# FFN rows turned by small DMAs in place of matmuls, down weights in four loads each, and an earlier row choice

## The chip, the cores and the metric

The kernel runs on one core of one Trainium2 chip. The metric is the device time of one execution in microseconds (us). Of the kernel before, three executions gave 251.94, 251.48 and 251.61 us, so the median is 251.61.

## The reference

One layer takes x (2048 tokens, 1024 features) and mixes two branches per token. Cut to what matters:

```python
g = sigmoid((x * gate_w).sum(-1, keepdims=True))       # one gate per token
q, k, v = split(x @ wqkv)                              # 32 heads of 32
pq, pk = phi(q), phi(k)                                # phi(t) = (t + 1 if t > 0 else exp(t)) + 1e-6
kv, z = sum_s(pk * v), sum_s(pk)
a = (pq @ kv) / (pq @ z + 1e-6) @ wo                   # linear attention
r = x @ w_r                                            # router
i = argmax(r)                                          # one row of 2048 is chosen
y = (silu(x[i] @ w_gate) * (x[i] @ w_up)) @ w_down     # FFN of this one row, 3584 wide
b = x;  b[i] += y * sigmoid(r[i])
out = g * a + (1 - g) * b
```

The FFN has three weight matrices of 7.3 MB each in bf16 and one row to multiply, so it is a matter of loading weights beside the attention's matmuls.

## The kernel before, in words

**Units.** The tokens are cut into 16 tiles of 128 (t = 0 to 15). A unit is eight matmuls of 128x512 into one PSUM buffer. `unit_KV(t, nb)` makes a quarter of k and v of tile t (nb 0 and 1: k, 2 and 3: v). `unit_Q(g, j)` makes a piece of q. k and q units are drained by two ScalarE activations (`u`, then `e`) and one VectorE step that writes `pk` or `pq_all`; v units by one ScalarE copy. Four PSUM buffers (`ps_work`) rotate among the units, so TensorE can start a unit once the unit some four places earlier is drained. `unit_KVACC(t)` adds pk and v of a tile into two accumulators; it runs for four tiles at a time, after the second unit of t = 8 and 12 and after the last tile. The tiles `pk` and `vt` have five buffers; GpSimd presets a column of each `vt` (a memset), and waits for that until `unit_KVACC` has freed the buffer.

**The order.** A loop over t from 4 to 15 emits four KV units and then a number of Q units per tile (`Q_PER_T`). Between the units it emits the FFN's work by tables: `GU_AFTER`, `GATE_STEPS`, `DOWN_STEPS`, `FLUSH_AFTER`. A place (t, i) is after KV unit i for i of 0 to 3, after Q unit i - 4 for i from 4 on, and "end" is the end of the tile. The helper `in_order` pins instructions to program order only while `strict[0]` is true. It is set false before the router, and from there on a scheduler chooses the place of most instructions in each engine's list by its own estimate of when inputs are ready; once built, each list runs as it stands.

**Row choice.** `router_part1` finds the best row on VectorE (`rmax`, `idx_i`), and GpSimd fetches that row (`xsel_row`, `xsel4`). `router_part2` turns it into columns on TensorE (`xs_ps`), copied to `xs_f` and `xs_pad`. The first weight load waits for the row fetch.

**FFN pieces.** All FFN weights come as pieces through one pool `ffw` of nine buffers, loaded on SP's queue in the order of `ffn_pieces`; a piece is loaded when the piece nine places earlier has been used.
- The first 2048 gate columns (half 0; four groups of 512) are multiplied on VectorE in 16 steps of 128x1024 (`gate_rows`, summed in `gacc`) and reduced over the partitions by TensorE (`gate_reduce`, `gps`).
- The up columns of half 0, and gate and up of half 1 (1536 columns) go over TensorE (`gate_up`): four matmuls side by side in 32 columns each, result on partitions 0, 32, 64 and 96 of one bank of `ps_ffn`. This pool has one buffer.
- `finish_gate` takes silu over a whole 128x512 tile (Exp on ScalarE, add, reciprocal and product on VectorE), though only four of its rows count. `finish_up` makes `h_bf`, and `h_transpose` brings h to 128 partitions with four or three matmuls against `sel4` into `hps`, copied to `hcol`.
- The 3584 rows of w_down are 28 slices of 128 rows, two per piece (`down_rows`); each slice is one VectorE step of 128x1024 into `yacc`, which is the first half of `gacc`. A piece is one load of 512 KB, in rows of 2 KB.
- `down_finish` sums `yacc` over the partitions on TensorE (`yps`), forms the row `brow` on VectorE and writes it into `xp`, a copy of x in DRAM made on SP's queue behind the down loads.

**After the FFN.** `zcol`, `kvbd` and `zc` are taken from the accumulators. `den_group` computes the denominators (`dps` on TensorE, `dn` on ScalarE, `rd` on VectorE); `unit_kvT` transposes kv (`pt`), `unit_M` multiplies with wo (`pm`), 15 more Q units run between, and the last loop makes the output tiles (`ot`). The tiles of this stage take over SBUF space of the earlier one: `dn` and `rd` may be written only when the transfer out of `brow` has landed. The third `pt` matmul needs a PSUM bank after `dn` has read it.

Of the kernel before, what the change touches and what calls it, by code (L numbers as in the profile page):

```python
# [13 lines left out]
BF = mybir.dt.bfloat16  # L14
F32 = mybir.dt.float32
I32 = mybir.dt.int32
U32 = mybir.dt.uint32
ALU = mybir.AluOpType
ACTF = mybir.ActivationFunctionType
# [3 lines left out]
P = 128  # L23
# [7 lines left out]
LN1EPS = math.log1p(EPS)  # L31
N_WARM = 6
Q_PER_T = {4: 2, 5: 1, 6: 1, 7: 2, 8: 1, 9: 1, 10: 2, 11: 1, 12: 1, 13: 1, 14: 1, 15: 0}
GU_AFTER = {(7, "end"): 4, (9, 1): 4, (10, 3): 8, (12, 1): 8}
FLUSH_AFTER = {(9, 3), (13, 0)}
GATE_STEPS = {6: 5, 7: 6, 8: 5}
M_AFTER = {3: (0, 0), 6: (0, 1), 9: (1, 0), 12: (1, 1)}
DOWN_STEPS = {10: (1, 1, 1, 1, 1, 1), 11: (1, 1, 1, 1, 1), 12: (1, 0, 1, 1, 1), 13: (1, 1, 1, 1, 1), 14: (1, 1, 1, 1, 1), 15: (1, 1, 1)}
FFN_DEPTH = 9
NORM_PER_T = [3, 2, 0, 2, 2, 2, 2, 2, 2, 2, 2, 0, 0, 0, 0, 0]  # L40

# [2 lines left out]
def kernel(  # L44
# [13 lines left out]
    nc = tc.nc  # L58
# [5 lines left out]
    const = ctx.enter_context(tc.tile_pool(name="const", bufs=1))  # L64
# [8 lines left out]
    strict = [True]  # L73
# [81 lines left out]
    nc.gpsimd.memset(one_bf[:], 1.0)  # L155
    ones_row = const.tile([1, P], BF)
    nc.gpsimd.memset(ones_row[:], 1.0)
    sel4 = const.tile([P, 4], BF)
    nc.gpsimd.memset(sel4[:], 0.0)
    for j in range(4):  # L160
        nc.gpsimd.memset(sel4[32 * j : 32 * j + 1, j : j + 1], 1.0)
    off16_i = const.tile([P, 1], I32)
    nc.gpsimd.iota(off16_i[:], pattern=[[0, 1]], base=0, channel_multiplier=16)
    wrg_pad = const.tile([P, KC, 32], BF)
# [3 lines left out]
    hcol = rt.tile([P, 28], F32)  # L168
# [193 lines left out]
    def router_part2():  # L362
        xs_ps = ps_ffn.tile([P, KC + 1], F32, tag="f")
        for c in range(KC):
            pe.matmul(xs_ps[:, c : c + 1], lhsT=xsel_row[0:1, c * P : (c + 1) * P], rhs=one_bf[0:1, 0:1],
                             start=True, stop=True)
        pe.matmul(xs_ps[:, KC : KC + 1], lhsT=ones_row[0:1, :], rhs=rmax_bf[0:1, 0:1], start=True, stop=True)
        dve.tensor_copy(xs_f[:], xs_ps[:, 0:KC])
        dve.tensor_copy(xs_pad[:, :, 0], xs_ps[:, 0:KC])
        act.activation(sig[:], xs_ps[:, KC : KC + 1], ACTF.Exp, scale=-1.0)  # L370
        dve.tensor_scalar_add(sig[:], sig[:], 1.0)
        dve.reciprocal(sig[:], sig[:])
    ffw = phq.enter_context(tc.tile_pool(name="ffw", bufs=FFN_DEPTH, side="right"))
    h_bf = [rt.tile([P, 512], BF, name=f"h_bf{i}") for i in range(2)]
    sg_t = [rt.tile([P, 512], F32, name=f"sg{i}") for i in range(2)]
    ffn_state = {}

    def gate_up_load(half, wmat, c):
# [8 lines left out]
        ffn_state["last_ld"] = ld  # L387
        return wt

    def finish_gate(half, ps, w):  # L390
        eg = tmp.tile([P, 512], F32, tag="ffn_e", bufs=1)
        act.activation(eg[:, 0:w], ps[:, 0:w], ACTF.Exp, scale=-1.0)
        dve.tensor_scalar_add(eg[:, 0:w], eg[:, 0:w], 1.0)
        dve.reciprocal(eg[:, 0:w], eg[:, 0:w])
        dve.tensor_tensor(sg_t[half][:, 0:w], ps[:, 0:w], eg[:, 0:w], op=ALU.mult)

    def finish_up(half, ps, w):
        dve.tensor_tensor(h_bf[half][:, 0:w], ps[:, 0:w], sg_t[half][:, 0:w], op=ALU.mult)

        def h_transpose():  # L400
            hps = ps_ffn.tile([P, 16], F32, tag="f")
            nb = w // P
            for b in range(nb):
                pe.matmul(hps[:, 4 * b : 4 * b + 4], lhsT=h_bf[half][:, b * P : (b + 1) * P], rhs=sel4[:], start=True, stop=True)
            dst = hcol[:].rearrange("p (j b) -> p j b", b=7)[:, :, 4 * half : 4 * half + nb]
            src = hps[:, 0 : 4 * nb].rearrange("p (b j) -> p j b", j=4)
            dve.tensor_copy(dst, src)

        ffn_state["pending"] = h_transpose

    def gate_up(half, which):
        w = 512 if half == 0 else 384
        for wi in which:
            wmat = (B_w_gate, B_w_up)[wi]
            for c in range(KC):
                def load(wmat=wmat, c=c):
                    return gate_up_load(half, wmat, c)

                def compute(wt, wi=wi, c=c):
                    if c == 0:  # L420
                        ps = ps_ffn.tile([P, 512], F32, tag="f")
                        ffn_state["ps"] = ps
                    ps = ffn_state["ps"]
                    for j in range(4):
                        pe.matmul(ps[32 * j : 32 * j + 32, 0:w], lhsT=xs_pad[:, c, :], rhs=wt[:, w * j : w * j + w],
                                  start=(c == 0), stop=(c == KC - 1), tile_position=(0, 32 * j))
                    if c == KC - 1:
                        (finish_gate, finish_up)[wi](half, ps, w)

                yield load, compute  # L430

# [14 lines left out]
    def gate_reduce():  # L446
        ps = ps_red.tile([P, 512], F32, name="gps")
        for j in range(4):
            pe.matmul(ps[32 * j : 32 * j + 32, :], lhsT=ones_f[:], rhs=gacc[:, 512 * j : 512 * j + 512],
                      start=True, stop=True, tile_position=(0, 32 * j))  # L450
        finish_gate(0, ps, 512)

    def down_rows():
        wdv = B_w_down.rearrange("(k p) n -> p k n", p=P)
        pairs = [(7 * j + b, 1) for b in (0, 2) for j in range(4)]
        pairs += [(7 * j + 4, 1) for j in range(4)] + [(6, 7), (20, 7)]
        for i2, (k0, dk) in enumerate(pairs):
            def load(k0=k0, dk=dk):
                wt = ffw.tile([P, 2048], BF, tag="ffw")
                ld = nc.sync.dma_start(out=wt[:].rearrange("p (k n) -> p k n", k=2), in_=wdv[:, k0 : k0 + dk + 1 : dk, :])  # L460
                tc.add_manual_dep(ld.ins, ffn_state["last_ld"].ins.name, NOSYNC, reason="queue order")
                ffn_state["last_ld"] = ld
                return wt

            def compute(wt, kk, i2=i2, k0=k0, dk=dk):
                w, h1 = wt[:, 1024 * kk : 1024 * kk + 1024], hcol[:, k0 + dk * kk : k0 + dk * kk + 1]
                if i2 == 0 and kk == 0:
                    dve.tensor_scalar(yacc, w, h1, None, op0=ALU.mult)
                else:
                    dve.scalar_tensor_tensor(yacc, w, h1, yacc, op0=ALU.mult, op1=ALU.add)  # L470

            yield load, compute
# [21 lines left out]
    def ffn_pieces():  # L494
        g0, u0, gu, dn = gate_rows(), gate_up(0, (1,)), gate_up(1, (0, 1)), down_rows()
        yield from islice(g0, 6)
        yield from islice(u0, 4)
        yield from g0
        yield from u0
        for n in (2, 4):  # L500
            yield from islice(dn, n)
            yield from islice(gu, 8)
        yield from dn
        yield from wo_pieces()

    pieces = ffn_pieces()
    inflight = deque()

    def ffn_prefetch():
        while len(inflight) < FFN_DEPTH:  # L510
            nxt = next(pieces, None)
            if nxt is None:
                return
            inflight.append((nxt[0](), nxt[1]))

    def ffn_flush():
        pend = ffn_state.pop("pending", None)
        if pend is not None:
            pend()

    def ffn_step(n):
        for _ in range(n):
            wt, comp = inflight.popleft()
            comp(wt)
            ffn_prefetch()
# [18 lines left out]
    def down_finish():  # L544
        ps = ps_ffn.tile([P, 256], F32, tag="f", name="yps")
        for j in range(4):
# [4 lines left out]
        nc.gpsimd.dma_start(out=xp[bass.ds(nonlocal_idx[0], 1), :].rearrange("o (j n) -> (o j) n", j=4),  # L551
                            in_=brow[0:128:32, :])

    q_units = deque((g, j) for j in range(4) for g in range(NG))
    for t in range(4):
        unit_KVACC(t)
    for t in range(4, NT):
        for nb in range(4):
            unit_KV(t, nb)
            if nb == 1 and t > 4 and t % 4 == 0:  # L560
                for t0 in range(t - 4, t):
                    unit_KVACC(t0)
            ffn_step(GU_AFTER.get((t, nb), 0))
            if (t, nb) in FLUSH_AFTER:
                ffn_flush()
            gate_step(int(nb < GATE_STEPS.get(t, 0)))
            steps = DOWN_STEPS.get(t, ())
            if nb < len(steps):
                down_step(steps[nb])
        for i in range(Q_PER_T[t]):  # L570
            unit_Q(*q_units.popleft())
            gate_step(int(4 + i < GATE_STEPS.get(t, 0)))
            if 4 + i < len(steps):
                down_step(steps[4 + i])
            if t == 4 and i == 0:
                router_part1()
                ffn_prefetch()
        if t == 5:
            router_part2()
        ffn_step(GU_AFTER.get((t, "end"), 0))  # L580
        if t == 8:
            gate_reduce()
    unit_Q(*q_units.popleft())
# [164 lines left out]
```

## Time and profile before

| what | value |
|---|---|
| median of three executions | 251.61 us |
| profiled execution, its own time | 251.87 us |
| span of its profile, first to last instruction | 250.1 us |
| TensorE busy | 244.7 us, 1602 matmuls |
| VectorE, ScalarE, GpSimd busy | 163.1, 125.8, 51.9 us |
| DMA: moved, mean rate | 47.73 MB, 191 GB/s |
| down loads: 14 of 512 KB, issue to landing (median) | 5.8 us |
| `wo` loads on SP: 8 of 128 KB, issue to landing (median) | 2.8 us |
| matmuls into `hps`, chain of waits | 0.08 us (four) and 0.05 us (three) |
| reciprocals of `finish_gate` on VectorE | 3.35 and 2.55 us |

The profile is of one execution and lies 0.26 us above the median. Its time is the span and 1.8 us around it. A group line names the engine, the operation, out<-in by the program's names, the shape and the count, then busy time and the mean of one in ns. In the timeline, a line has the start in us, the length, engine, operation, and in brackets the idle time of the engine before it and what ended that. The view of waits has: who waited <- for whom: us in total, times, longest. The chain in order of time has: start, length, what. L80 is the helper that records the order, so instructions are told apart by their tiles.

### The profile page before, as it was taken

The page shows a single profiled execution, that of the slowest core. Times are in us where ns is not written, and L with a number is a line of the kernel's source. Part 1 is how long each engine was busy: PE and PEld are TensorE (multiplying, and loading weights), DVE is VectorE, ACT ScalarE, POOL GpSimd, SP SyncE. Part 2 cuts the span into 40 slices and gives each one's busy share as a digit, 9 for nine tenths or more (in the row PEclk, how much of TensorE's full clock was granted, in tenths as well). Part 3 has the DMA queues.
Part 4 walks back from the last instruction along what each step waited for, and adds up shares of the span by engine and source line. Part 5 has one row for each costly group of instructions (what it writes and reads, how often), then busy time and mean ns, then how long its engine had stood idle before and what let it go on. Part 6 is the DMA issues. An engine that isn't in the chain of part 4 may idle for free.

```text
span 250.1 us, 4197 instructions
## 1 busy us (share of the span) xinstructions
PE 244.7 (98%) x1602; PEld 111.1 (44%) x1602; DVE 163.1 (65%) x257; ACT 125.8 (50%) x200; POOL 51.9 (21%) x102
## 2 busy tenths in 40 slices
PE   7999999999999999999999999999999999999994
PEld 3444454444444434444544444444444444444442
DVE  0045015326999288699689993585878999953442
ACT  2096235556545364564535554568887633333210
POOL 5000001010000100000132000210666689950000
PEclk9999999999999999999999999999999999999999
DMA  6999990019999928499699996230000564454122
GB/s 199 303 340 225 258 334 26 0 27 320 350 348 272 340 58 250 146 338 327 194 292 300 457 349 134 70 132 1 3 0 5 171 210 144 161 175 144 66 84 84
DMA packets 47242, 47.73 MB, mean 191 GB/s; under 512 B 18732, under 2 KB 35380, under 8 KB 47160
## 3 DMA queue, kind: packets, MB, share of 16 engines
q1 hardware_dynamic: 46552, 46.29, 60.7%
q0 software_dynamic: 640, 1.19, 1.8%
q8 instruction: 12, 0.20, 0.3%
q14 instruction: 6, 0.05, 0.1%
q10 hardware_dynamic: 32, 0.00, 0.0%
HBM read 39.34 MB, written 8.40 MB: 191 GB/s over the span
## 4 chain that ended last, share of the span: by engine, by line
PE 95%; DMA 2%; SPq 1%; DVE 0%; issue 0%; DVEq 0%
PE ps L80 88%; PE first L80 2%; DMA wkv<-in_A_wqkv_dram 2%; PE kvacc L80 2%; PE dps L80 1%; PE rps L80 1%; SPq L80 1%; PE pm L80 1%; PE gps L80 0%; DVE ot L80 0%; PE yps L80 0%; PE xs_ps L80 0%; DVEq L743 0%; PE pt L80 0%; PE hps L80 0%
## 5 line engine op out<-in xcount | busy, mean ns | idle before, releaser
L80 PE MATMUL ps<-wkv,xT 128*128 128x512 bf16 x480 | 106.5, 379 | 0.0
L80 PEld LDWEIGHTS <-xT 128*128 128x128 bf16 x512 | 49.3, 98 | 60.5 <-issue 2.6
L80 PE MATMUL ps<-xT,wq 128*128 128x512 bf16 x256 | 58.4, 379 | 0.0
L80 PE MATMUL ps<-m_sb,pq_all 128*128 128x512 bf16 (+2 forms) x264 | 55.6, 373 | 0.0
L80 ACT ACTIVATE u<-ps 128x512 f32<-128x512 f32 x60 | 35.9, 599 | 36.5 <-PE ps L80 35.8
L80 ACT ACTIVATE e<-u 128x512 f32<-128x512 f32 x64 | 40.4, 632 | 2.0
L646 POOL TENSOR_TENSOR pq_all<-pq_all,rb 128x512 bf16<-128x512 bf16 x32 | 36.6, 1163 | 14.4 <-DVE rb L80 13.9
L80 PEld LDWEIGHTS <-pq_all 128*128 128x128 bf16 x264 | 25.5, 98 | 30.2 <-issue 0.4
L80 PEld LDWEIGHTS <-wq 128*128 128x128 bf16 x256 | 24.3, 98 | 30.2 <-issue 2.1
L80 DVE SCALAR_TENSOR_TENSOR pq_all<-ps,e 128x512 bf16<-128x512 f32 x32 | 22.0, 686 | 23.6 <-ACT e L80 23.5
L80 DVE SCALAR_TENSOR_TENSOR gacc<-wt,hcol,gacc 128x1024 f32<-128x1024 bf16 x27 | 34.6, 1281 | 4.1 <-DMA wt<-in_B_w_down_dram 3.7
L80 ACT CAST vt<-ps 128x512 bf16<-128x512 f32 x32 | 18.9, 589 | 32.8 <-PE ps L80 32.8
L80 DVE SCALAR_TENSOR_TENSOR ot<-ps,gate,xg 128x512 bf16<-128x512 f32 (+2 forms) x33 | 23.6, 724 | 15.1 <-PE ps L80 14.2
L80 ACT ACTIVATE xg<-xt,omg 128x1024 f32<-128x1024 bf16 x16 | 18.2, 1148 | 25.8 <-DVE ot L80 25.8
L80 DVE SCALAR_TENSOR_TENSOR pk<-ps,e 128x512 bf16<-128x512 f32 x28 | 19.1, 686 | 7.5 <-ACT e L80 7.5
L209 POOL MEMSET vt<- 128x16 bf16 x16 | 2.4, 200 | 101.8 <-PE kvacc L80 101.3
L80 DVE STREAM_SHUFFLE rb<-rdp 128x512 f32<-128x512 f32 x32 | 22.5, 731 | 0.0
L80 DVE SCALAR_TENSOR_TENSOR gacc<-wt,xs_f,gacc 128x1024 f32<-128x1024 bf16 x14 | 17.4, 1283 | 0.3 <-DMA wt<-in_B_w_gate_dram 0.3
L80 DVE CAST r_bf<-rps 128x512 bf16<-128x512 f32 x1 | 0.7, 692 | 12.6 <-PE rps L80 12.6
L80 DVE SCALAR_TENSOR_TENSOR pk<-first,e 128x512 bf16<-128x512 f32 x4 | 2.8, 692 | 8.4 <-ACT e L80 8.4
L80 PE MATMUL first<-wkv,xT 128*128 128x512 bf16 x32 | 7.4, 379 | 0.2
L80 DVE RECIPROCAL rd<-dn 128x512 f32<-128x512 f32 x2 | 6.7, 3334 | 0.0
(104 smaller groups left out, 88.1 us busy)
## 6 DMA issues: line engine op xcount, KB each, us to landing
wt<-in_B_w_down_dram SPq DMA_DIRECT2D x14, 512.0 KB, 5.8
wt<-in_B_w_gate_dram SPq DMA_DIRECT2D x8, 512.0 KB, 7.2
wt<-in_B_w_up_dram SPq DMA_DIRECT2D x8, 512.0 KB, 8.9
xt<-xp SPq DMA_DIRECT2D x16, 256.0 KB, 2.9
out_dram<-ot SPq DMA_DIRECT2D x15, 256.0 KB, 2.0
wt<-in_B_w_gate_dram SPq DMA_DIRECT2D x8, 384.0 KB, 5.3
wt<-in_B_w_up_dram SPq DMA_DIRECT2D x8, 384.0 KB, 7.5
wkv<-in_A_wqkv_dram SPq DMA_DIRECT2D x8, 256.0 KB, 5.2
```

The lines of the kernel that those rows point to most:

```text
L80: inst = fn(*a, **k)
L209: nc.gpsimd.memset(vt_t[t][:, :, :, 64:65], 1.0)
L646: nc.gpsimd.tensor_tensor(sl, sl, rb[:], op=ALU.mult)
```

## The change

1. `sel4`, `h_transpose`, `finish_gate`, `finish_up` and the flushes go. In their place `finish` copies the tile to SBUF on ScalarE (`rows`), and a DMA on GpSimd's queue spreads its four rows that count over 128 partitions (`cols`, 16 or 12 columns). `silu` and `product` then work on 128x16 or 128x12 and are emitted at the places in `FINISH_AT`, pinned in order there.
2. Column f of a group of h now lies on another partition, so the down rows are regrouped to match: each piece is loaded by four DMAs of 32 partitions, 128 KB each, in rows of 4 KB.
3. `router_part1` moves from after the first Q unit of t = 4 to place (4, 1), `router_part2` from the end of t = 5 to (5, 0).
4. The tables change: the gate steps begin at t = 5, the up pieces of half 0 go to (7, 3) and the end of t = 8, the down steps begin at t = 9 and end at (15, 3); the second group of down loads has three pieces in place of four.

```diff
-GU_AFTER = {(7, "end"): 4, (9, 1): 4, (10, 3): 8, (12, 1): 8}
-FLUSH_AFTER = {(9, 3), (13, 0)}
-GATE_STEPS = {6: 5, 7: 6, 8: 5}
+GU_AFTER = {(7, 3): 4, (8, "end"): 4, (10, 3): 8, (12, 1): 8}
+GATE_STEPS = {5: (0, 1, 1, 1, 1), 6: (1, 1, 1, 1, 1), 7: (1, 1, 1, 0, 1, 1), 8: (1, 1)}
-DOWN_STEPS = {10: (1, 1, 1, 1, 1, 1), 11: (1, 1, 1, 1, 1), 12: (1, 0, 1, 1, 1), 13: (1, 1, 1, 1, 1), 14: (1, 1, 1, 1, 1), 15: (1, 1, 1)}
+DOWN_STEPS = {9: (0, 0, 0, 1, 1), 10: (1, 1, 0, 0, 1, 1), 11: (1, 1, 1, 1), 12: (0, 0, 1, 1, 1), 13: (1, 1, 1, 1, 2), 14: (1, 1, 1, 1, 1), 15: (1, 1, 1, 1)}
+FINISH_AT = {(9, 2), (11, 0), (12, 4)}
...
+    def finish(wi, half, ps):
+        w = 512 if half == 0 else 384
+        n = w // 32
+        act.copy(rows[wi][:, 0:w], ps[:, 0:w])
+        nc.gpsimd.dma_start(out=cols[half][wi][:, 0:n], in_=rows[wi][0:128:32, 0:w])
+        g, u, h = cols[half][0][:, 0:n], cols[half][1][:, 0:n], slice(16 * half, 16 * half + n)
+
+        def silu():
+            e = rt.tile([P, 16], F32, name=f"ffn_e{half}")
+            act.activation(e[:, 0:n], g, ACTF.Exp, scale=-1.0)
+            dve.tensor_scalar_add(e[:, 0:n], e[:, 0:n], 1.0)
+            dve.reciprocal(e[:, 0:n], e[:, 0:n])
+            dve.tensor_tensor(g, g, e[:, 0:n], op=ALU.mult)
+
+        def product():
+            dve.tensor_tensor(h_bf[:, h], u, g, op=ALU.mult)
+            dve.tensor_copy(hcol[:, h], h_bf[:, h])
+
+        late.append((silu, product)[wi])
...
     def down_rows():
-        wdv = B_w_down.rearrange("(k p) n -> p k n", p=P)
...
+        wdv = B_w_down.rearrange("(j f) n -> j f n", j=4)
+        for k in range(0, 28, 2):
+            c0, n, i0 = (0, 16, k) if k < 16 else (512, 12, k - 16)
...
-                ld = nc.sync.dma_start(out=wt[:].rearrange("p (k n) -> p k n", k=2), in_=wdv[:, k0 : k0 + dk + 1 : dk, :])
+                src = wdv[:, c0 : c0 + 32 * n, :].rearrange("j (r i) n -> j r i n", i=n)[:, :, i0 : i0 + 2, :]
+                for j in range(4):
+                    ld = nc.sync.dma_start(out=wt[32 * j : 32 * j + 32, :].rearrange("p (i n) -> p i n", i=2), in_=src[j])
...
-        for n in (2, 4):
+        for n in (2, 3):
             yield from islice(dn, n)
             yield from islice(gu, 8)
         yield from dn
...
+    def slot(t, i):
+        gu = GU_AFTER.get((t, i), 0)
+        ffn_step(gu)
+        strict[0] = True
+        while late and (t, i) in FINISH_AT:
+            late.popleft()()
+        strict[0] = False
+        for step, plan in ((gate_step, GATE_STEPS), (down_step, DOWN_STEPS)):
+            steps = plan.get(t, ())
+            if i != "end" and i < len(steps):
+                step(steps[i])
...
+            if (t, nb) == (4, 1):
+                router_part1()
+                ffn_prefetch()
+            if (t, nb) == (5, 0):
+                router_part2()
+            slot(t, nb)
         for i in range(Q_PER_T[t]):
             unit_Q(*q_units.popleft())
-            gate_step(int(4 + i < GATE_STEPS.get(t, 0)))
-            if 4 + i < len(steps):
-                down_step(steps[4 + i])
-            if t == 4 and i == 0:
-                router_part1()
-                ffn_prefetch()
-        if t == 5:
-            router_part2()
-        ffn_step(GU_AFTER.get((t, "end"), 0))
+            slot(t, 4 + i)
+        slot(t, "end")
```

More of the change, by code (lines that the diff above doesn't have):

```diff
@@ L157 @@
     nc.gpsimd.memset(ones_row[:], 1.0)
[L158 to L161, printed above, removed]
     off16_i = const.tile([P, 1], I32)
@@ L373 @@
     ffw = phq.enter_context(tc.tile_pool(name="ffw", bufs=FFN_DEPTH, side="right"))
-    h_bf = [rt.tile([P, 512], BF, name=f"h_bf{i}") for i in range(2)]
-    sg_t = [rt.tile([P, 512], F32, name=f"sg{i}") for i in range(2)]
+    rows = [rt.tile([P, 512], F32, name=f"gu_rows{i}") for i in range(2)]
+    cols = [[rt.tile([P, 16], F32, name=f"gu_cols{i}{h}") for i in range(2)] for h in range(2)]
+    h_bf = rt.tile([P, 28], BF)
     ffn_state = {}
@@ L388, in gate_up_load @@
         return wt
[L390 to L409, printed above, removed]
+    def finish(wi, half, ps):
[14 more added lines that the diff above has]
+        late.append((silu, product)[wi])
     def gate_up(half, which):
@@ L427, in compute @@
                     if c == KC - 1:
-                        (finish_gate, finish_up)[wi](half, ps, w)
+                        finish(wi, half, ps)
                 yield load, compute
@@ L450, in gate_reduce, with load, compute @@
                       start=True, stop=True, tile_position=(0, 32 * j))
-        finish_gate(0, ps, 512)
+        finish(0, 0, ps)
+        late.rotate(1)
     def down_rows():
-        wdv = B_w_down.rearrange("(k p) n -> p k n", p=P)
[L455 to L458, printed above, removed]
-                wt = ffw.tile([P, 2048], BF, tag="ffw")
-                ld = nc.sync.dma_start(out=wt[:].rearrange("p (k n) -> p k n", k=2), in_=wdv[:, k0 : k0 + dk + 1 : dk, :])
-                tc.add_manual_dep(ld.ins, ffn_state["last_ld"].ins.name, NOSYNC, reason="queue order")
-                ffn_state["last_ld"] = ld
-                return wt
-            def compute(wt, kk, i2=i2, k0=k0, dk=dk):
-                w, h1 = wt[:, 1024 * kk : 1024 * kk + 1024], hcol[:, k0 + dk * kk : k0 + dk * kk + 1]
-                if i2 == 0 and kk == 0:
+        wdv = B_w_down.rearrange("(j f) n -> j f n", j=4)
+        for k in range(0, 28, 2):
+            c0, n, i0 = (0, 16, k) if k < 16 else (512, 12, k - 16)
+            def load(c0=c0, n=n, i0=i0):
+                wt = ffw.tile([P, 2048], BF, tag="ffw")
+                src = wdv[:, c0 : c0 + 32 * n, :].rearrange("j (r i) n -> j r i n", i=n)[:, :, i0 : i0 + 2, :]
+                for j in range(4):
+                    ld = nc.sync.dma_start(out=wt[32 * j : 32 * j + 32, :].rearrange("p (i n) -> p i n", i=2), in_=src[j])
+                    tc.add_manual_dep(ld.ins, ffn_state["last_ld"].ins.name, NOSYNC, reason="queue order")
+                    ffn_state["last_ld"] = ld
+                return wt
+            def compute(wt, kk, k=k):
+                w, h1 = wt[:, 1024 * kk : 1024 * kk + 1024], hcol[:, k + kk : k + kk + 1]
+                if k + kk == 0:
                     dve.tensor_scalar(yacc, w, h1, None, op0=ALU.mult)
@@ L507 @@
     inflight = deque()
+    late = deque()
     def ffn_prefetch():
@@ L514, in ffn_prefetch @@
             inflight.append((nxt[0](), nxt[1]))
[L516 to L519, printed above, removed]
     def ffn_step(n):
@@ L562 @@
                     unit_KVACC(t0)
[L563 to L569, printed above, removed]
+            if (t, nb) == (4, 1):
[4 more added lines that the diff above has]
+            slot(t, nb)
         for i in range(Q_PER_T[t]):
             unit_Q(*q_units.popleft())
-            gate_step(int(4 + i < GATE_STEPS.get(t, 0)))
-            if 4 + i < len(steps):
-                down_step(steps[4 + i])
-            if t == 4 and i == 0:
-                router_part1()
-                ffn_prefetch()
-        if t == 5:
-            router_part2()
-        ffn_step(GU_AFTER.get((t, "end"), 0))
+            slot(t, 4 + i)
+        slot(t, "end")
         if t == 8:
```

## The prediction

> **What bounds the kernel now.** I read the shares of the chain that ended last, then TensorE's own waits, then the chain in order of time, then VectorE's, ScalarE's and GpSimd's timelines about the one place where TensorE needs the FFN's result.
>
> ```profile
> PE 95%; DMA 2%; SPq 1%; DVE 0%; issue 0%; DVEq 0%
> ```
> ```profile
> PE warm_ps L80 <- PEq L732: 1.0, 1, 1.0
> PE pst L80 <- DMA xnat<-in_A_x_dram: 0.7, 1, 0.7
> ```
>
> TensorE is the chain, and after its first microseconds it waits for nothing. So the gain to be had is only the TensorE work removed, and every wait that TensorE gets is paid in full. Now the place where one can arise:
>
> ```profile
> 155.84 1.14 PE kvacc L80 x64
> 156.98 0.57 PE yps L80 x8
> 157.55 3.56 PE ps L80 x16
> 161.11 0.98 PE dps L80 x16
> 162.09 1.83 PE ps L80 x8
> 163.92 0.22 PE pt L80 x32
> 164.14 5.29 PE ps L80 x24
> ```
>
> `yps` sums the down rows that VectorE has added up in `gacc`. VectorE beside it:
>
> ```profile
> 144.94 5.24 DVE L80 SCALAR_TENSOR_TENSOR gacc<-wt,hcol,gacc 128x1024 f32<-128x1024 bf16 x4
> 150.09 0.68 DVE L80 SCALAR_TENSOR_TENSOR pq_all<-ps,e 128x512 bf16<-128x512 f32 x1
> ...
> 157.17 0.69 DVE L80 SCALAR_TENSOR_TENSOR pq_all<-ps,e 128x512 bf16<-128x512 f32 x1 [4.49 <-ACT e L80]
> 157.78 0.22 DVE L80 COPY zcol<-kvacc 128x4 f32<-128x4 f32 x2
> 157.91 0.41 DVE L80 CAST kvbd<-kvacc 128x256 bf16<-128x256 f32 x1
> 158.25 0.47 DVE L80 SCALAR_TENSOR_TENSOR brow<-yps,sig,xsel 128x256 bf16<-128x256 f32 x1
> 158.64 0.17 DVE L80 TENSOR_SCALAR gate<-gate 128x16 f32<-128x16 f32 x1
> ```
>
> The last down step ends at 150.2, 6.8 us ahead of `yps`; four of them take 5.24, so 1.31 each. After `yps` comes a short chain that in this kernel ends before anybody asks: `brow`, its write into `xp` by GpSimd, and `dn` on ScalarE, which stands behind that write because the two share SBUF space:
>
> ```profile
> 159.01 0.60 POOL L551 DMA_DIRECT2D xp<-brow  x1 [22.58 <-DVE gate L80]
> ```
> ```profile
> 162.31 0.67 ACT L80 ACTIVATE dn<-dps,eps_t 128x512 f32<-128x512 f32 x1
> ```
>
> **What the Trainium skill says.** (1) "TensorE: Matmul & The Clock Gate", Architectural detail (the array is 16 of 32x32): VectorE and ScalarE are strict FIFOs, and TensorE pulls only weight loads ahead. So a step that stands late in VectorE's list is late, ready or not; the trace of before runs in the listed order throughout. (2) The same page, Part 1: after an idle window of about 3.4 us the TensorE clock falls to half, and a busy window of that length brings it back. The trace fits at its start: six 512-wide warm-up matmuls take 2.72 us, 0.45 each, against 0.216 later. (3) "DMA: Bandwidth & Descriptors", Rules for kernel authors: splitting one load over partitions brings no bandwidth. No run here shows that yet.
>
> **The built order of the changed kernel.** Most of this part of the kernel is placed by the scheduler, so I listed what it made. VectorE's end of the FFN, with the places in its list:
>
> ```
> 112 pk15<-ps_1810                 (second unit of t=15)
> 113-114 gacc<-wt_1538 x2          (down piece 4 of the last 9)
> 115 pq_all<-ps_1847               (the Q unit ahead of kvacc)
> 116-120 zcol x2, kvbd, zc, kvbd
> 121-122 gacc<-wt_1547 x2
> 123-124 pq_all<-ps_1937, ps_1951  (the Q units after kvacc)
> 125-132 gacc<-wt_1556, 1565, 1574, 1585 x2 each
> 133 brow<-yps
> ```
>
> On TensorE `yps` now stands behind Q, Q, `dps`, Q and the first two `pt` matmuls. The built waits: `yps` for step 132; `dn` for the landing of `xp<-brow`; the third `pt` matmul for `dn`.
>
> **The sum, part by part.**
>
> *Removed on TensorE.* The h transposes, 0.08 + 0.05 us in the chain: -0.13. One visit to the FFN's 32-column layout (now at the end of t=8) adjoins the gate reduction, which has that layout too. A visit costs 0.2: by the start times of the matmuls 309 ns on entry and about as much on leaving against 216, 0.09 to 0.12 each. So -0.2. VectorE loses the wide reciprocals (3.35 and 2.55) and their companions, some 8 us; it has idle time there, so nothing follows.
>
> *Added on TensorE.* The list splits the last eight up pieces (after `kvacc` of t=12) into six visits between matmuls of three units, where before made one: 5 x 0.2 = +1.0.
>
> *Row choice sooner.* Before, `rmax` ran at 48.35; now it stands behind the `pk` that ended at 43.25, so it, the row fetch and the first nine weight loads come 5.15 sooner (`c` landed at 41.8, no wait). `xs_ps` comes 4 units sooner: 4 x 1.73 = 6.9, so 49.85, with the row landed at 53.53 - 5.15 = 48.4: no wait. But the weights are now 1.8 later against TensorE. Pieces 1 and 2 landed at 58.36 and 60.90, now 53.2 and 55.75. VectorE sits at its first gate step until 53.3, then at the third until 55.77. From there its list has that step, a `pk`, four steps and the `pq` of t=5; at the pitches of before (step 1.20, `pk` 0.61) this `pq` starts at 55.77 + 1.20 + 0.61 + 4 x 1.20 = 62.4 and ends at 63.05. Its PSUM buffer is wanted by unit (6,3) at 49.85 + 0.31 + 7 x 1.73 = 62.3: a wait of 0.8. The seventh gate piece (75.37 - 5.15 = 70.2) holds the next `pq` to 72.1 against 71.7: 0.4. Together +1.3, bounds 0 and 2.5.
>
> *Small DMAs and copies.* Four ScalarE copies (0.59 by the `rg_f` copy) replace two Exps; ScalarE is at 50%. GpSimd issues four gathers, 0.6 to 0.7 each, landing 1.6 to 2.5 after issue by the `c` and `xsel` rows. From the end of t=8 to their use after (9,2) are three units, 5.2 us, against 0.6 x 2 + 0.7 x 2 + 2 = 4.6; TensorE runs some units further on its four buffers if they are late. In GpSimd's queue they stand behind `vt` memsets whose `kvacc` is done by then. 0; at worst 0.5.
>
> *Down loads in four.* SP issues 56 loads where it had 14. The 128 KB `wo` loads cost SP 0.38 to 0.60 each and landed 2.1 to 2.8 later. The last nine pieces wait for a step at about 124.5: 36 x 0.43 = 15.5, so issued by 140, landed by 143. VectorE asks for the fifth of them at 161. Hidden by 18 us. `xp<-x2d` queues behind: 140 in place of 128.52; it took 24.2 beside other loads, so 164 at worst, wanted at 176. Hidden.
>
> *The tail.* TensorE reaches `yps`'s old place at 156.98 - 0.13 - 0.2 + 1.0 + 1.3 = 158.95. Place 115 starts 1.33 after its unit (155.84 to 157.17 in before): 157.8 + 1.33 = 159.15. Then 0.6, then 116 to 120 at 1.1 (157.78 to 159.49 without the steps between): 160.85. Two steps at 1.31: 163.5. Two `pq` at 0.6: 164.7. Eight steps, 10.5: 175.2. TensorE has run its Q, Q, `dps`, Q by 166.4 and stands. `yps` 0.57: 175.8; `brow` 0.5: 176.3; issue 0.3 after it: 176.6; landing 1.65: 178.3; `dn` 0.75: 179.05; the rest of `pt`: 179.3, where before had 164.14. That is +15.2, of which 2.0 was there before the tail. Nothing takes it back: TensorE had no slack after it. Behind the waiting `dn` stand ScalarE's Exps of the next Q unit, behind step 132 VectorE's `gate`, `rd` (3.34) and the same unit's `pq`, behind `xp<-brow` GpSimd's last four `wo` loads; TensorE stands as well, and asks for `rd` and these `wo` four and nine units later, 7 and 15 us: no more is added.
>
> *The clock.* An idle of 12 us with 0.6 of work in it outlasts the window of point 2. `yps` at half clock +0.4; then 3.4 to 6.8 us at half speed lose 1.7 to 3.4 (estimate from the skill's window). I take 2.0, as the start of the span suggests the short end. +2.4.
>
> Sum: +17.6. On the profiled execution, 251.87 with a span of 250.1, that is 269.5; it lies 0.26 above the median of 251.61, so 269.2.
>
> **Rivals.** (a) *Late weights.* Four small loads per piece, each waiting for the eighth load before it to land: if a piece takes 6 us in place of 1.7, the last lands at 124.5 + 54 + 2.5 = 181, two steps follow, and the time is some 277. It decides from 5.2 us a piece. Against: a 512 KB load landed 3 us after issue when alone. (b) *A shorter tail.* `dn` doesn't stand behind the row write, or the clock doesn't fall: 3 or 2.4 less, 266 to 267. (c) *Not slower.* The order run is the order written by hand, not the listed one: the last down step would then follow the last unit but one and end 1.5 us ahead of `yps`, and the visits stay whole. Only -0.33 remains, 251.3, if the gate weights also land 1.3 sooner than I have it; otherwise 252.6. Decisive is whether steps 121 to 132 run before `kvacc` ends. Against it: in before, list and trace agree.
>
> **How the numbers follow.** Forecast 0.78, (a) 0.07, (b) 0.11, (c) 0.04, of which 0.02 faster. What I count as no change is within 0.2%, 0.5 us, about what a measurement can tell. The range, 265.3 to 272.3, holds the forecast with its bounds (early waits -1.3 to +1.2, gate-step pitch 1.20 in place of 1.31 giving -1.1, clock -0.7 to +1.4) and (b).
>
> **What would show it.** In the changed profile: one wait of TensorE before `yps` of about 9 us, ended by `gacc` on VectorE, and one of about 3 before `pt` ended by `dn`; eight `gacc` steps in one run from about 165 to 175; a lowered TensorE clock in the slice after it; waits of under 1 us at about 62 and 72. Wrong, if `yps` comes within 5 us of `kvacc`, or if VectorE's idle time in the tail ends on DMA `wt`.

## The result, and the profile after

The changed kernel takes 268.49 us (median of four executions, 268.13 to 269.56), the kernel before 251.75 us beside it (251.48 to 251.94). The ratio is 1.0669, with a 95% interval from 1.0644 to 1.0694: 6.7% slower, 16.7 us. The profiled execution of the changed kernel took 268.13 us, with a span of 266.6 us against 250.1.

TensorE's own waits in the changed kernel (who waited <- for whom: us in total, times, longest):

```profile
PE yps L80 <- DVE gacc L80: 8.7, 1, 8.7
PE pt L80 <- ACT dn L80: 3.6, 1, 3.6
PE pst L80 <- DMA xnat<-in_A_x_dram: 1.1, 1, 1.1
PE warm_ps L80 <- PEq L731: 1.0, 1, 1.0
PE dps L80 <- DVE pq_all L80: 0.7, 1, 0.7
```

The last but one was there before, and so, shorter, was the wait for `xnat` at the start. The first two and the last are new, and all three lie within 20 us of each other. TensorE's timeline there (start, length, engine, line, operation, count, and in brackets the idle time before it and what ended it):

```profile
156.79 1.21 PE L80 MATMUL kvacc<-vt,pk 128*64 128x65 bf16 x64
...
165.33 0.19 PE L80 MATMUL pt<-ident,kvbd 32*32 32x32 bf16 x2
174.23 1.08 PE L80 MATMUL yps<-gacc,ones_f 128*32 128x256 f32 x8 [8.71 <-DVE gacc L80]
178.86 0.31 PE L80 MATMUL pt<-ident,kvbd 32*32 32x32 bf16 x30 [3.56 <-ACT dn L80]
```

`yps` followed `kvacc` at once in the kernel before; now it comes 17.4 us after the start of `kvacc`. VectorE in the same stretch:

```profile
158.20 0.69 DVE L80 SCALAR_TENSOR_TENSOR pq_all<-ps,e 128x512 bf16<-128x512 f32 x1 [1.98 <-ACT e L80]
158.80 0.22 DVE L80 COPY zcol<-kvacc 128x4 f32<-128x4 f32 x2
...
159.94 2.60 DVE L80 SCALAR_TENSOR_TENSOR gacc<-wt,hcol,gacc 128x1024 f32<-128x1024 bf16 x2
162.45 1.28 DVE L80 SCALAR_TENSOR_TENSOR pq_all<-ps,e 128x512 bf16<-128x512 f32 x2
163.65 10.52 DVE L80 SCALAR_TENSOR_TENSOR gacc<-wt,hcol,gacc 128x1024 f32<-128x1024 bf16 x8
175.43 0.48 DVE L80 SCALAR_TENSOR_TENSOR brow<-yps,sig,xsel 128x256 bf16<-128x256 f32 x1 [1.26 <-PE yps L80]
```

Ten down steps stand behind `zcol`, and no bracket there names a transfer: the weights are in place, VectorE simply reaches the steps late. After `brow` the row has to be written, and only then may `dn` run. GpSimd's and ScalarE's timelines:

```profile
176.21 0.60 POOL L546 DMA_DIRECT2D xp<-brow  x1 [29.97 <-DVE gate L80]
```
```profile
178.12 0.69 ACT L80 ACTIVATE dn<-dps,eps_t 128x512 f32<-128x512 f32 x1 [15.16 <-DMA xp<-brow]
```

The stretches of this time (bounds, length, busy time of TensorE, its weight loads, VectorE, ScalarE and GpSimd with counts, granted TensorE clock, DMA share, GB/s):

```profile
166.00:175.00 9.00, 0.77 (x8) 0.20 (x8) 7.96 (x7) 0.00 (x0) 0.00 (x0) 0.65 0.00 0
175.00:179.00 4.00, 0.45 (x34) 0.23 (x30) 1.15 (x5) 0.88 (x2) 2.62 (x5) 0.50 0.20 54
179.00:182.00 3.00, 2.67 (x36) 1.10 (x26) 3.00 (x1) 1.15 (x4) 1.10 (x3) 0.50 1.00 280
```

In the first, VectorE alone works until `yps` starts at 174.23 (TensorE's 0.77): no other engine, and no DMA. In the third, TensorE is busy again at half clock. The shares of the chain that ended last are a poor guide here:

```profile
PE 66%; DMA 19%; issue 8%; DVE 4%; ACT 1%; POOLq 0%; SPq 0%; DVEq 0%; ACTq 0%; POOL 0%
```

"DMA 19%" reads as if transfers were the loss. The chain is followed back from the last instruction through whatever released each step, here from the row write to the copy of x that it writes into, and on to the down loads ahead of that copy; it tells of a path, not of who waits. TensorE's waits and VectorE's brackets name no transfer in this place; ScalarE's names one, the row write, which landed 1.7 us after issue.

To compare kernels stage by stage I cut the span at the starts of TensorE's instructions: A from the first `kvacc` (tiles 0 to 3) to that at t = 8, B to that at t = 12, C to the last `kvacc`, D from there to the second group of `dps`. The edges are at 36.46, 80.64, 121.95, 155.77 and 193.69 us before, and at 36.53, 80.99, 121.95, 156.79 and 210.28 us after. Each ratio is to executions of the kernel before that ran beside the kernel in its row.

| kernel | A | B | C | D | median | ratio to before, 95% interval |
|---|---|---|---|---|---|---|
| before | 44.18 | 41.31 | 33.82 | 37.92 | 251.75 | |
| changed | 44.46 | 40.96 | 34.84 | 53.49 | 268.49 | 1.0669 (1.0644 to 1.0694) |
| e2_one_load | 44.50 | 40.96 | 38.05 | 37.91 | 254.54 | 1.0104 (1.0088 to 1.0121) |
| e3_before_four | 44.18 | 41.31 | 35.46 | 53.24 | 268.88 | 1.0683 (1.0665 to 1.0701) |
| e4_brow_keep | 44.73 | 40.97 | 34.84 | 51.02 | 266.05 | 1.0580 (1.0556 to 1.0603) |
| e6_pin_dvepe | 45.00 | 40.97 | 37.19 | 46.16 | 263.72 | 1.0480 (1.0462 to 1.0497) |
| e8_pin_through | 44.90 | 40.97 | 37.39 | 42.82 | 260.35 | 1.0343 (1.0316 to 1.0370) |
| e11_pin_zcol | 44.50 | 40.96 | 37.20 | 37.91 | 254.71 | 1.0134 (1.0095 to 1.0173) |
| e12_pin_zcol_steps | 44.85 | 41.03 | 42.22 | 37.92 | 259.67 | 1.0327 (1.0291 to 1.0362) |
| e9_contig_steps | 44.18 | 40.96 | 33.74 | 37.92 | 251.33 | 0.9989 (0.9974 to 1.0004) |
| e10_old_row_choice | 44.18 | 42.12 | 34.12 | 37.91 | 252.54 | 1.0028 (1.0005 to 1.0052) |

Of the change's 16.5 us of span, D has 15.57, C 1.02, A 0.28, and B gives 0.35 back.

### The profile page after: what moved, and what is told of

Its sections match the earlier page's. It is cut to its first block, busy times and chain, and to the rows that moved or that the text cites. A ratio compares the mean times of both kernels' runs of the same rounds, so it can differ in the third digit from the quotient of the medians.

```text
span 266.6 us, 4219 instructions
## 1 busy us (share of the span) xinstructions
PE 246.2 (92%) x1568; PEld 111.3 (42%) x1595; DVE 157.3 (59%) x257; ACT 127.1 (48%) x204; POOL 54.2 (20%) x101
## 4 chain that ended last, share of the span: by engine, by line
PE 66%; DMA 19%; issue 8%; DVE 4%; ACT 1%; POOLq 0%; SPq 0%; DVEq 0%; ACTq 0%; POOL 0%
PE ps L80 60%; DMA xp<-in_A_x_dram 6%; DMA wt<-in_B_w_gate_dram 5%; DMA wt<-in_B_w_down_dram 5%; PE first L80 2%; DVE gacc L80 2%; DMA xnat<-in_A_x_dram 2%; PE kvacc L80 1%; DVE pk L80 1%; PE rps L80 1%; DMA xsel<-in_A_x_dram 1%; DMA xp<-brow 1%; PE pm L80 1%; PE dps L80 0%; PE gps L80 0%
## 5 line engine op out<-in xcount | busy, mean ns | idle before, releaser
L80 PE MATMUL ps<-xT,wq 128*128 128x512 bf16 x249 | 59.3, 386 | 0.9 <-issue 0.6
L80 ACT ACTIVATE dn<-dps,eps_t 128x512 f32<-128x512 f32 x2 | 1.4, 688 | 17.4 <-DMA xp<-brow 15.2
L80 PE MATMUL yps<-gacc,ones_f 128*32 128x256 f32 x8 | 1.1, 635 | 8.7 <-DVE gacc L80 8.7
L391 POOL DMA_DIRECT2D gu_cols<-gu_rows x4 | 2.8, 688 | 31.0 <-ACT gu_rows L80 31.0
```

Of the source, the lines that this page charges most:

```text
L80: inst = fn(*a, **k)
L391: nc.gpsimd.dma_start(out=cols[half][wi][:, 0:n], in_=rows[wi][0:128:32, 0:w])
```

## The experiments

My theory: the four loads hurt through the list and not through the wire. The scheduler expects the down pieces late, sets ten steps behind `zcol`, and TensorE pays in D. Rivals: the loads' own time, the small DMAs' latency, the sooner row choice, and the wait of `dn` behind the row write.

**One load for a piece (e2_one_load).** Rows of W_down other than the reference's meet h in this kernel.

```diff
-                for j in range(4):
-                    ld = nc.sync.dma_start(out=wt[32 * j : 32 * j + 32, :]..., in_=src[j])
+                src = B_w_down[128 * k : 128 * k + 256, :].rearrange("(p i) n -> p i n", i=2)
+                ld = nc.sync.dma_start(out=wt[:].rearrange("p (i n) -> p i n", i=2), in_=src)
```

> The changed kernel with one load of 512 KB for each down piece (256 contiguous rows, two for each partition) in place of four of 128 KB; small DMAs and row choice stay as changed. The rows of W_down that meet h are others than the reference's, so y of the chosen row differs; bytes, shapes and the number of steps are the same. In the built order no down step stands behind kvacc's end, yps follows kvacc, and half 1 of up is one visit. Main theory (the loss is the order that the four loads bring): 251.0 to 252.5 us, as before or up to 0.5 below; no wait of TensorE over 1.2 us in the last phase. Rival (the small DMAs or the sooner row choice carry the loss): 260 us or more, with waits for gu_cols or gate weights in front of TensorE.

254.54 us: all of the loss in D is gone with the four loads, but 2.7 us remain, and I had missed them. They lie in C (4.2 over the kernel before in the profiled execution, which took 255.62). VectorE's timeline of e2_one_load has them:

```profile
123.56 1.28 DVE L80 SCALAR_TENSOR_TENSOR gacc<-wt,hcol,gacc 128x1024 f32<-128x1024 bf16 x1 [3.46 <-DMA wt<-in_B_w_down_dram]
...
130.97 5.25 DVE L80 SCALAR_TENSOR_TENSOR gacc<-wt,hcol,gacc 128x1024 f32<-128x1024 bf16 x4 [3.73 <-DMA wt<-in_B_w_down_dram]
```

The changed step plan fetches five down pieces ahead of the last eight up pieces, where six went ahead before. The sixth now queues behind the up loads, and the built wait of the next load is for this piece's second step, whose buffer it takes (the step ends at 126.64, the load is issued at 126.67). So VectorE waits twice, and a `pq` behind four late steps holds TensorE for 2.31 us up to 136.87. In the changed kernel this cost did not show: VectorE's list has no down step from 123.58 to 137.29, so nothing there waits for these pieces.

**Four loads in the kernel before (e3_before_four).**

```diff
-                ld = nc.sync.dma_start(out=wt[:].rearrange("p (k n) -> p k n", k=2), in_=wdv[:, k0 : k0 + dk + 1 : dk, :])
+                for j in range(4):
+                    ld = nc.sync.dma_start(out=wt[32 * j : 32 * j + 32, :].rearrange("p (k n) -> p k n", k=2),
+                                           in_=wdv[32 * j : 32 * j + 32, k0 : k0 + dk + 1 : dk, :])
```

> The kernel before with one thing changed: each down load is split into four loads of 32 partitions; h still goes through matmuls, the row choice stays where it was. In the built order ten down steps stand behind kvacc's end, yps behind the first two pt, and the up visits of half 1 fall apart into single pieces. Main theory: 267.5 to 270 us, the whole loss of the change, with yps waiting 8 to 9 us for gacc and pt 3 to 4 us for dn. Rival (the small DMAs or the row choice): within 2 us of 251.7.

268.88 us, within the interval of the changed kernel's ratio. TensorE's waits:

```profile
PE yps L80 <- DVE gacc L80: 9.7, 1, 9.7
PE pt L80 <- ACT dn L80: 3.5, 1, 3.5
```

This one edit, without small DMAs and with the old row choice, makes the whole loss; the rivals for those two fall. The wait for `yps` is 0.7 above what I expected, and C holds 1.64 for the up visits, now in single pieces.

**`brow` in memory of its own (e4_brow_keep).**

```diff
-        brow = rt.tile([P, 256], BF, name="brow")
+        brow = keep.tile([P, 256], BF, name="brow")
```

> The changed kernel with brow in memory of its own, so that dn need not wait until the copy xp<-brow has landed; the order of the lists is the changed kernel's. Main theory: only the second of TensorE's two late waits goes (3.6 us) and with it a part of the half clock after it; yps still waits 8 to 9 us: 264.0 to 265.8 us. Rival (the shared memory is the mechanism, the late steps are not): 256 us or less. Rival (dn waits for something else): no change, 268.5 us.

266.05 us, a little over the range. `yps` waits 8.7 us as in the changed kernel, and `pt` still 1.4 where I expected none. ScalarE's timeline ("issue" means that the profile shows nothing it waited for):

```profile
175.66 0.69 ACT L80 ACTIVATE dn<-dps,eps_t 128x512 f32<-128x512 f32 x1 [13.03 <-issue]
```

`brow` is computed from 175.10 on, and `dn` starts 0.08 us after its end at 175.58. By the built waits `dn` still stands behind that step, presumably for the other row tiles that it reads, which lie in the old place. So the landing is worth 2.2 us of the loss (1.0669 against 1.0580); it is a second effect, behind the late `yps`.

**The list put back, every transfer kept (e6, e8, e11).** A flag pins VectorE and TensorE to program order from t = 12 on; e8 keeps it until `kvbd` is copied; e11 also writes the `zcol`, `zc`, `kvbd` block ahead of the last two Q units.

```diff
-                if last[0] is not None and strict[0]:
+                if last[0] is not None and (strict[0] or pin[0] and engine is not nc.scalar):
...
+        pin[0] = t >= 12
```

> The changed kernel, every load and small DMA as it is, with VectorE and TensorE held to program order from place 12 on, so that the down steps stand among the work of the places and none behind kvacc's end but the last two. Main theory (order, not transfers): yps waits 1 to 3 us, dn 3 to 4 us for xp<-brow, no stall over 4 us: 254 to 258 us. Rival (the four loads land too late for the steps, whatever the order): VectorE waits for wt in places 13 to 15 and holds TensorE back before kvacc's end, 262 us or more.

> The changed kernel with every load and small DMA as it is (four loads for each down piece), VectorE and TensorE held to program order from place 12 on until kvbd is copied. VectorE's built list is then the one of the kernel before: all down steps in their places, zcol after them, yps straight after kvacc, and half 1 of up in one visit. Theory (order, not transfers): the stall of yps and that of pt are gone, 252 to 256 us; what is left over the kernel before are waits of VectorE for down pieces that land behind the up loads (2 to 3 us in the run with one load). Rival (the four loads cost the time themselves): VectorE waits for wt in places 13 to 15 as well, and the time is 260 us or more.

> As e8_pin_through, and zcol, zc and kvbd written ahead of the last two Q units in the program, so that the fixed order no longer holds dps behind two evictions of Q. All loads and small DMAs stay as changed (four loads for each piece). Theory (order): of e8_pin_through the wait of 3.3 us for kvbd and about 1.5 us of half clock behind it go, and the rest over the kernel before is what the run with one load also had (2.7 us): 254.5 to 256.5 us. Rival (four loads cost several us by themselves): 258 us or more, with VectorE waiting for wt after 132 us.

The first two missed, and each by waits that the pin itself made. In e6_pin_dvepe `zcol`, which was not pinned, went ahead of a `pk` that the last `kvacc` needs, and VectorE stood 9.55 us before it. In e8_pin_through `zcol` came after the VectorE steps of two Q units, and `dps` waited 3.3 us. With both mended, e11_pin_zcol takes 254.71 us, in the range. Its TensorE timeline:

```profile
158.97 1.21 PE L81 MATMUL kvacc<-vt,pk 128*64 128x65 bf16 x64
160.11 0.64 PE L81 MATMUL yps<-gacc,ones_f 128*32 128x256 f32 x8
160.68 3.63 PE L81 MATMUL ps<-xT,wq 128*128 128x512 bf16 x16
164.24 1.05 PE L81 MATMUL dps<-pq_all,zc 128*32 128x512 bf16 x16
```

D is 37.91, as in the kernel before, though all 56 down loads of 128 KB are in this kernel. By the ratios, (1.0669 - 1.0134) x 251.7, putting the lists back wins 13.5 of the 16.8 us. VectorE's last wait for a weight in e11_pin_zcol ends at 128.83; the sixteen steps after that pair find their data, the last ending at 158.1:

```profile
128.83 2.61 DVE L81 SCALAR_TENSOR_TENSOR gacc<-wt,hcol,gacc 128x1024 f32<-128x1024 bf16 x2 [4.83 <-DMA wt<-in_B_w_down_dram]
...
154.20 3.91 DVE L81 SCALAR_TENSOR_TENSOR gacc<-wt,hcol,gacc 128x1024 f32<-128x1024 bf16 x3
```

So the pieces did arrive in time. That the cut of the loads moves the lists is shown by e2 and e3; that it does so through an estimate of late arrival is my reading, since no view shows the scheduler's estimates. Of the 3.4 us that C still has over the kernel before, 2.8 are four waits of TensorE for `vt`, which all pinned kernels have and no other; I take them for the pin's own cost, without having isolated it. I had put this rest down to the step plan with five pieces, as in e2_one_load, so that the time fell into the range is luck in part: VectorE did wait 4.83 us for a piece, but TensorE's waits for `pq_all` come to only 0.2.

**The step plan of before, from t = 11 on, under four loads (e12_pin_zcol_steps).**

```diff
-DOWN_STEPS = {..., 11: (1, 1, 1, 1), 12: (0, 0, 1, 1, 1), 13: (1, 1, 1, 1, 2), 14: (1, 1, 1, 1, 1), 15: (1, 1, 1, 1)}
+DOWN_STEPS = {..., 11: (1, 1, 1, 1, 1), 12: (1, 0, 1, 1, 1), 13: (1, 1, 1, 1, 1), 14: (1, 1, 1, 1, 1), 15: (1, 1, 1)}
-        for n in (2, 3):
+        for n in (2, 4):
```

> As e11_pin_zcol, and six down pieces in place of five are fetched and consumed ahead of the up visit of half 1, by the step plan of the kernel before. Everything that the change adds is in it: four loads for each piece, small DMAs, the sooner row choice. Theory (order and step plan, not transfers): VectorE's wait of 4.8 us for a down piece near 129 us falls under 3 us and TensorE keeps its pace: 251.8 to 254.0 us. Rival (the four loads' landing or issue is a cost of its own): 255.5 us or more, VectorE waiting for wt more than 4 us in all after 122 us.

259.67 us: a miss, and the rival has a part of the truth. VectorE's wait for a down piece fell only from 4.8 to 3.0 us, and TensorE met a new one:

```profile
125.02 0.35 PE L81 MATMUL ps<-wt,xs_pad 128*32 128x384 bf16 x4 [0.79 <-DMA wt<-in_B_w_up_dram]
127.47 0.35 PE L81 MATMUL ps<-wt,xs_pad 128*32 128x384 bf16 x4 [2.11 <-DMA wt<-in_B_w_up_dram]
127.75 5.30 PE L81 MATMUL ps<-wkv,xT 128*128 128x512 bf16 x16
```

These two waits, and 1.7 us at half clock in the 16 matmuls behind them, are 4.6 of the 5.0 us by which C is longer than in e11_pin_zcol. SP's queue says why the up weights came late: four pieces took it 7.75 us here, almost all of it issue, against 4.91 in the kernel before, of which 3.1 were a wait for a free buffer. The eight up loads began at 112.06 against 106.78 (2.4 us of this were there when the pieces began). First this kernel, then the kernel before:

```profile
104.13 7.75 SPq L460 DMA_DIRECT2D wt<-in_B_w_down_dram  x16
112.06 11.49 SPq L379 DMA_DIRECT2D wt<-in_B_w_up_dram  x8
```
```profile
101.77 4.91 SPq L460 DMA_DIRECT2D wt<-in_B_w_down_dram  x4
106.78 11.89 SPq L381 DMA_DIRECT2D wt<-in_B_w_up_dram  x8
```

So four loads are free only while nothing urgent is queued behind them. The changed kernel's plan with five pieces ahead avoids this; with one load a piece it costs what e2_one_load showed.

**A regrouping that needs one load (e7, e9, e10).** If half 0 takes columns 0 to 2047 and half 1 the rest, the row 16p+i (or 2048+12p+i) belongs to partition p, and one load brings a piece. e9 adds the step plan shown above for e12; e10 also takes row choice, gate steps and first visits back to the old places.

```diff
-        w, c0 = (512, 0) if half == 0 else (384, 512)
+        w, c0 = (512, 0) if half == 0 else (384, 2048)
...
-                               in_=wmat[c * P : (c + 1) * P, :].rearrange("p (j f) -> p j f", j=4)[:, :, c0 : c0 + w])
+        ld = nc.sync.dma_start(out=wt[:, 0 : 4 * w], in_=wmat[c * P : (c + 1) * P, c0 : c0 + 4 * w])
...
-            c0, n, i0 = (0, 16, k) if k < 16 else (512, 12, k - 16)
+            c0, n, i0 = (0, 16, k) if k < 16 else (2048, 12, k - 16)
+                src = B_w_down[c0 : c0 + P * n, :].rearrange("(p i) n -> p i n", i=n)[:, i0 : i0 + 2, :]
```

> The changed kernel with its halves cut elsewhere: half 0 of gate and up takes columns 0 to 2047 and half 1 the rest, so that row 16p+i (or 2048+12p+i) belongs to partition p and one load takes a whole down piece; the gate and up loads become 4 KB or 3 KB runs for each partition in place of four of 1 KB or 768 B. The plan of steps is the changed kernel's. Theory: the built lists are those of the run with one load, so 253.5 to 255 us, with VectorE again waiting about 3.5 us for the down piece behind the up loads; if the longer runs make the up loads land sooner, up to 1 us less. Rival (the transfers' shape matters more than the order): under 252.5 us or over 256 us.

> As e7_contig, and six down pieces in place of five are fetched and consumed ahead of the up visit of half 1, by the step plan of the kernel before; the small DMAs and the sooner row choice stay. Theory: the waits of 3.5 and 3.7 us for down pieces near 123 and 131 us shrink to those of the kernel before (1.8 and under 1), and what TensorE lost behind them (2.7 us) goes: 251.0 to 252.0 us. Rival (the small DMAs or the row choice cost it): 253.5 us or more, as with five pieces.

> As e9_contig_steps, and the row choice, the gate steps and the first FFN visits go back to the places of the kernel before; of the change only the small DMAs in place of matmuls are left (with one load for a down piece). Theory: the sooner row choice costs 0.3 us, and without it and without the h transposes and the extra visit (0.33 us) this is 251.0 to 251.7 us, at most 0.5 under e9_contig_steps. Rival (the small DMAs' 4 to 6 us to landing hold TensorE): over 252.5 us, with TensorE waiting behind h_bf or ffn_e.

e7_contig takes 252.79 us, ratio 1.0035 (1.0013 to 1.0058): under the range, 1.7 us faster than e2_one_load with the same step plan. The longer runs of the gate and up loads are the main difference between the two; where they save it is not shown, since the one profile of e7_contig is of an execution of 255.51 us, far above its median. e9_contig_steps takes 251.33 us beside 251.72: as fast as the kernel before, and not shown to be faster, since the interval reaches 1.0004. From e7_contig to here only the step plan differs, so five pieces in place of six cost 1.2 us by the ratios. TensorE is the chain again:

```profile
PE 98%; DVE 0%; DVEq 0%; issue 0%
```

This kernel has the small DMAs and the sooner row choice, and A, B and C add up to 0.43 us less than before. So the two are no loss in this kernel; whether its longer runs cover a small one is open. e10_old_row_choice at 252.54 us missed, and the other way: with row choice, gate steps and first visits in the old places it is 1.2 us slower than e9_contig_steps. There h is ready late (its first down step starts at 101.17, against 96.85 in e9_contig_steps and 96.56 before), the buffers of the first down pieces come free late, and TensorE waits 0.7 us for gate weights near 106. I had put the finish steps of e10 one place later than the old flush, so a part of this, not measured apart, is my own choice.

## Why the prediction was right

Forecast 269.2, measured 268.49, and the mechanism is the forecast's: list order, then `yps`, then `brow`, the row write and `dn`, then the clock.

- *Removed on TensorE, -0.33.* B fell by 0.35, and by 0.28 to 0.35 in all kernels with the change's early part. Right.
- *Six visits, +1.0.* C rose by 1.02. Right.
- *Row choice sooner, +1.3.* Mis-sized, the largest error. A rose by 0.28, one gap of 496 ns at 70.7 in place of 216. The wait of 0.8 near 62 rested on the second gate piece landing at 55.75; VectorE took it at 54.33, after both steps of the first, without a wait, and the `pq` that should have ended at 63.05 was done by 61.6. The 0.4 near 72 rested on the seventh piece at 70.2; VectorE had it at 69.24, and the gap at 70.7 is what is left of this wait:

```profile
52.40 0.75 DVE L80 TENSOR_SCALAR gacc<-wt,xs_f 128x1024 f32<-128x1024 bf16 x1 [1.20 <-DMA wt<-in_B_w_gate_dram]
...
53.67 0.74 DVE L80 TENSOR_SCALAR gacc<-wt,xs_f 128x1024 f32<-128x1024 bf16 x1
54.33 1.28 DVE L80 SCALAR_TENSOR_TENSOR gacc<-wt,xs_f,gacc 128x1024 f32<-128x1024 bf16 x1
...
60.91 0.69 DVE L80 SCALAR_TENSOR_TENSOR pq_all<-ps,e 128x512 bf16<-128x512 f32 x1
...
69.24 1.28 DVE L80 SCALAR_TENSOR_TENSOR gacc<-wt,xs_f,gacc 128x1024 f32<-128x1024 bf16 x1 [0.47 <-DMA wt<-in_B_w_gate_dram]
```

  I had shifted the old landings by 5.15 us. The loads started 5.54 sooner (48.25 against 53.79), and SP issued the first six in 4.32 us against 5.69; why they went faster I have not tested. The six other kernels with this part and these gate loads have 0.3 to 0.8 more in A (44.50 to 45.00 against 44.18), so the lower half of my bounds was the place to be.
- *Small DMAs, 0.* The cost is right, the size behind it wrong: a gather landed 1.6 to 2.5 us after issue in my sum, and 3.8 to 6.1 in the run (issues: KB each, median us to landing):

```profile
gu_cols<-gu_rows POOLq DMA_DIRECT2D x2, 8.0 KB, 6.1
gu_cols<-gu_rows POOLq DMA_DIRECT2D x2, 6.0 KB, 4.3
```

  VectorE did wait for one, and TensorE's four buffers hid it, as the forecast had it for late ones:

```profile
135.79 0.17 DVE L80 TENSOR_TENSOR h_bf<-gu_cols,gu_cols 128x12 bf16<-128x12 f32 x1 [2.81 <-DMA gu_cols<-gu_rows]
```

- *Down loads in four, hidden.* Issue took 19.76 us for 36 loads (15.5 forecast), so the last landed near 148 and not 143; VectorE took the fifth piece at 159.94 and the sixth at 163.65. Right: the loads were hidden, and only the built list set steps back behind them. Rival (a), a piece slower than 5.2 us, was far off: 2.2 us a piece.
- *The tail.* The chain from 159.15 to 179.3 came out as 158.20 to 179.2, each step nearly as long as forecast (eight steps 10.52 against 10.5). It starts sooner by the 1.0 us that the early waits lacked.
- *The clock, +2.4.* `yps` took 1.08, against 0.64 in e11_pin_zcol, so +0.4; the first six Q matmuls, until 182.1, ran at 427 ns. From the start of `pt` to the first `pm` the loss is about 1.6 (7.1 us against 5.5 in the kernel before) where I took 2.0. The Trainium skill's page "TensorE: Matmul & The Clock Gate", Part 1, has the busy window at about 3.4 us; the time at half clock after `pt` was 3.2 here.
- *Rival (c), the order as written.* The time I gave it, 252.6, was too low: e11_pin_zcol runs nearly that order, with `zcol` moved, at 254.71. I had not counted the four waits for `vt` in C that the pinned order has.

Errors in the sum: -1.0 for the early waits, -0.4 for the clock, and some tenths the other way, together the -1.1 of span by which the forecast (17.6) was over the run (16.5).

## What to carry to other kernels

Where a scheduler places instructions, a change in how a load is cut can change the lists of engines that only wait for it: here one edit of the loads moved ten steps of VectorE. Read the built order before counting bytes, and test it by keeping the transfers and pinning the list. A loss that shows as a wait on one engine can hide another plan's cost; when the first is mended, look for the second in the stage before it. And a regrouping of rows is best chosen so that one load still covers all partitions: here another cut of the halves gave that at no cost.

## What the runs showed of the hardware

- A GpSimd gather of 8 or 6 KB from four partitions to 128 landed 3.8 to 6.1 us after issue in the changed kernel. The fixed part in the Trainium skill's page "DMA: Bandwidth & Descriptors", Anatomy of one DMA, is about 2.0 us; these ran beside weight loads, with the DMA engines 63 to 100% busy, and I take the rest for queueing, untested.
- The same page's Rules for kernel authors hold that halves of the partitions in separate loads share the same engines and bring nothing. No run measures the bandwidth alone; VectorE's wait for a down piece near 129 was 3.0 us with four loads (e12_pin_zcol_steps), and near 124 it was 1.8 with one (before), so no gain shows. The runs add a price: a piece in four loads of 128 KB took SP 1.9 to 2.6 us (7.75 us for four and 20.48 for eight in e12_pin_zcol_steps), where one load of 512 KB took 0.42 (median, kernel before).
- With gate and up loads in runs of 4 KB or 3 KB a partition, stage A was 44.18 with the sooner row choice, and 44.46 to 45.00 with runs of 1 KB or 768 B: VectorE's wait for a gate piece near 69 us, 0.47 in the changed kernel, was gone in e9_contig_steps.
- TensorE's granted clock fell to 0.50 for about 3.4 us after waits of 0.79 and 2.11 us with 0.35 us of work between them (e12_pin_zcol_steps), and stayed at 1.00 after a single wait of 2.31 us (e2_one_load).
